# The last projection of a decode kernel in two half rows: two column groups, two PSUM banks, two copies, one store

## The chip, the cores and the metric

The kernel runs on one core of one Trainium2 chip. The metric is device time in microseconds for one launch; the median of several runs is compared. Beside the runs there is one profiled execution, from which all durations of single instructions come.

## What is computed

One decode step of a single token with 512 features. The token is normalised, goes through sliding-window attention over the last 4096 cached positions (32 query heads, 8 key and value heads of 128) and through a gated feed-forward part of 1792 hidden features, and everything is added up:

```
xn  = layernorm(x)                                   # 1 x 512
q   = xn @ wq                                        # 1 x 4096 = 32 heads of 128
o   = softmax(q k^T * 128**-0.5) v                   # last 4096 positions of the caches
A   = o @ wo                                         # 4096 x 512
r   = xn @ w_r                                       # one number
y   = (silu(xn @ w_gate) * (xn @ w_up)) @ w_down     # 512 x 1792, 512 x 1792, 1792 x 512
out = x + A + xn + y * sigmoid(r)                    # 1 x 512, bf16
```

With one token the choice among tokens in the reference always picks it, so the routed part is the plain sum above.

## The kernel before

All weights and the caches' window are read once from HBM, 30.67 MB, and the transfers are issued by SyncE (SP) in the order in which they are used: wq, keys, values, w_gate and w_up, wo, w_down. wo is read in four pieces of eight rows (of its 32) and w_down in five pieces of 4, 4, 3, 2 and 1 rows (of its 14); a row here is a block of 128 partitions by 512 columns, and row j multiplies column j of the transposed activation. Into the SBUF space of the keys go wo (`wo_sb`) and w_down (`wd_sb`), so their transfers are issued when the keys have been copied on.

The program is not scheduled by a planner: every engine has its own list of instructions in the order in which the Python code calls it, and the order between engines is kept by semaphores. `PE.mark(ins)` lets an instruction count up TensorE's semaphore and returns a token, and `DVE.need(token)` puts a wait for it into VectorE's list, ahead of everything that follows there. PE is TensorE, DVE is VectorE, ACT is ScalarE, POOL is GpSimd.

The stage that the change touches is the last one. All its matmuls have a stationary operand of a single column (one token), so each one yields a single row of output; to use more of the array, matmuls are placed with `tile_position` in one of four groups of 32 columns, where they write to PSUM partition 0, 32, 64 or 96. There are two patterns:

- `grouped` (L495): row j of a weight, all 512 columns, goes to column group j mod 4. Four rows of the weight run in four groups, and the sum over the groups is left for later. The target is `a_ps`, PSUM bank 5. The 32 rows of wo and the rows 0 to 7 of w_down are done like this.
- `by_columns` (L500): one row is cut into four pieces of 128 columns, and each piece goes to its own group, so nothing has to be added over the groups. The target is `g_ps`, 128 columns of PSUM bank 0. The rows 8 to 13 of w_down are done like this.

In between, at L517, DVE adds `rf` (which holds x + xn in partition 0 and zero elsewhere) to `a_ps` and leaves `part` in SBUF, fp32. PE then multiplies `part` by `sel4`, a column which has a one at partitions 0, 32, 64 and 96, through `by_columns` too: that adds the four groups up and brings them into `g_ps`. It stands in PE's list after the third piece of w_down (k == 2). Both banks are set to zero with a zero matmul ahead of the stage (L488, L489), and `fill` (L155) issues matmuls of zeros which only keep PE busy.

At the end DVE copies `g_ps`, 128 partitions by 128 columns, to `res` as bf16 (L527), and SP stores the four rows at partitions 0, 32, 64 and 96 as the 512 outputs (L529; the helper that issues all transfers is at L159). POOL waits for that store.

Of the kernel before, what the change touches and what calls it, by code (L numbers as in the profile page):

```python
# [38 lines left out]
def kernel(  # L39
# [15 lines left out]
    P = 128  # L55
    D = A_x.shape[2]
# [9 lines left out]
    FB = F // P  # L66
# [18 lines left out]
    kT = sb("kT", [P, 4, 1024], BF16)  # L85
# [8 lines left out]
    hTr = sb("hTr", [P, FB, 32], BF16)  # L94
# [5 lines left out]
    zst = sb("zst", [P, P], BF16)  # L100
    zmov = sb("zmov", [P, 512], BF16)
# [5 lines left out]
    sel4 = sb("sel4", [P, 1], F32)  # L107
# [13 lines left out]
    oT2 = sb("oT2", [P, RJ], BF16)  # L121
# [7 lines left out]
    ps = nc.alloc_psum_tensor("ps", [P, 8, 512], F32)  # L129
# [4 lines left out]
    pT_ps = ps[:, 0:2, :].bitcast(BF16)  # L134
    pv_ps = ps[:, 2, :]
    a_ps = ps[:, 5, :]
    g_ps = ps[:, 0, 0:P]
    rf = kT[:, 0, :].bitcast(F32)
    part = kT[:, 1, :].bitcast(F32)
    res = kT[:, 2, 0:P]  # L140

    wq_flat = wq_sb[:].rearrange("p a b -> p (a b)")
    wgu = wq_flat[:, 0:2 * KT * F]
# [1 line left out]
    wd_sb = k_flat[:, 0:FB * D]  # L145
    wo_sb = k_flat[:, FB * D:(FB + RJ) * D]

    S = lambda n: nc.alloc_semaphore(n)
    PE, ACT, DVE, POOL, SP = (Eng(nc, nc.tensor, "pe"), Eng(nc, nc.scalar, "act"), Eng(nc, nc.vector, "dve"),
                              Eng(nc, nc.gpsimd, "pool"), Eng(nc, nc.sync, "sp"))  # L150
    te, ac, ve, gp, sy = nc.tensor, nc.scalar, nc.vector, nc.gpsimd, nc.sync

    def fill(n):
        for _ in range(2 * n):
            te.matmul(ps[:, 7, :], lhsT=zst[:], rhs=zmov[:], start=True, stop=True)  # L155

    def dma(eng, name, out_, in_):
        s = S("d_" + name)
        eng.dma_start(out=out_, in_=in_).then_inc(s, 16)  # L159
        return (s, 16)  # L160
# [36 lines left out]
    a = DVE.mark(ve.bn_stats(out=stats[:], in_=xrow[:]))  # L197
# [6 lines left out]
    a = DVE.mark(ve.reciprocal(out=sml[:, 1:2], in_=sml[:, 0:1]))  # L204
# [5 lines left out]
    for kt in range(KT):  # L210
        ins = te.matmul(ps[:, 6, 256 + kt:257 + kt], lhsT=xn_row[:].rearrange("a (p k) -> a k p", k=KT)[:, kt, :],  # L211
                        rhs=ident_bf[0:1, 0:1], start=True, stop=True)
# [5 lines left out]
    with nc.allow_low_precision(reason="0/1 values are exact in bf16"):  # L218
# [4 lines left out]
                                     in_=ident_bf[:].rearrange("p (q h) -> p h q", h=2)))  # L223
# [23 lines left out]
    for kh in range(2):  # L247
# [4 lines left out]
        for hf in range(2):  # L252
            for kt in range(kh * KH, (kh + 1) * KH):
                for c in range(4):
                    ins = te.matmul(ps[32 * c:32 * c + 1, hf, :], lhsT=xnT[:, kt:kt + 1],  # L255
                                    rhs=wq_sb[:, kt, (4 * hf + c) * 512:(4 * hf + c + 1) * 512],
                                    start=(kt == 0), stop=(kt == KT - 1), tile_position=(0, 32 * c))
# [4 lines left out]
    for hf in range(2):  # L262
# [3 lines left out]
        for hl in range(4):  # L266
            ins = te.transpose(qT_ps[:, hl, :], q4[:, hf, hl * DH:(hl + 1) * DH], ident_bf[:])  # L267
# [76 lines left out]
    with te.Fori(1, 9) as i:  # L344
# [14 lines left out]
    wd_chunks = [(0, 4), (4, 8), (8, 11), (11, 13), (13, 14)]  # L359
    t_wd = [dma(sy, f"wd{k}", wd_sb[:, j0 * D:j1 * D], wd_v[:, j0 * D:j1 * D]) for k, (j0, j1) in enumerate(wd_chunks)]  # L360
# [4 lines left out]
    a = POOL.mark(gp.memset(rf, 0.0))  # L365
# [8 lines left out]
    a = DVE.mark(ve.reduce_max(out=gm[:], in_=ps[0:2, 6, 0:P].rearrange("a (q c) -> a c q", q=8), axis=AX.X))  # L374
# [6 lines left out]
                              start=True, stop=True))  # L381
# [6 lines left out]
    for h in range(2):  # L388
        PE.need(t_p[h])
        for k in range(8):  # L390
            ins = te.transpose(tp[:, h, k * P:(k + 1) * P], p_sb[:, h, k * P:(k + 1) * P], ident_bf[:])
# [39 lines left out]
    with te.Fori(1, 9) as i:  # L431
# [4 lines left out]
        for tl in range(4):  # L436
            ins = te.matmul(pv_ps[32 * tl:32 * tl + 32, :], lhsT=pTcur[:, tl].rearrange("p q e r -> p (q e r)"),  # L437
                            rhs=vin[:, 0].rearrange("p (q t) d -> p t q d", t=4)[:, tl],
                            start=True, stop=False, tile_position=(0, 32 * tl))
        ins.then_inc(pe_pva, 1)  # L440
        te.wait_ge(s_vb, i)
        for tl in range(4):
            ins = te.matmul(pv_ps[32 * tl:32 * tl + 32, :], lhsT=pTcur[:, 4 + tl].rearrange("p q e r -> p (q e r)"),  # L443
                            rhs=vin[:, 1].rearrange("p (q t) d -> p t q d", t=4)[:, tl],
                            start=False, stop=True, tile_position=(0, 32 * tl))
        ins.then_inc(pe_pv, 1)
        collect(psf[:, bass.ds(4 * 512 + g * 8, 8)]).then_inc(pe_col, 1)
        for _ in range(W3):
# [9 lines left out]
    a = DVE.mark(ve.reduce_sum(out=oT_f[:].rearrange("p (g j) -> p g j", g=HP),  # L458
                               in_=ps[:, 4, 8:72].rearrange("p (g u j) -> p g j u", g=HP, u=2), axis=AX.X))
# [7 lines left out]
    for m in range(2):  # L467
        PE.need(t_g if m == 0 else t_u)
        for kt in range(KT):
            for c in range(4):  # L470
                ins = te.matmul(ps[32 * c:32 * c + 1, 2 + m, 0:FC], lhsT=xnT[:, kt:kt + 1],
                                rhs=wgu[:, m * KT * F + kt * F + c * FC:m * KT * F + kt * F + (c + 1) * FC],
                                start=(kt == 0), stop=(kt == KT - 1), tile_position=(0, 32 * c))
# [6 lines left out]
    a = ACT.mark(ac.activation(out=gth4[:], in_=ps[:, 2, 0:FC], func=ACTF.Tanh, scale=0.5))  # L480
# [5 lines left out]
    DVE.need(t_h)  # L486
    t_hT = DVE.mark(ve.transpose(out=hTr[:].rearrange("p b i -> p (b i)"), in_=h4[:].rearrange("p b i -> p (b i)")))
    te.matmul(a_ps, lhsT=zst[:], rhs=zmov[:], start=True, stop=False, skip_group_check=True)  # L488
    te.matmul(g_ps, lhsT=zst[:], rhs=zmov[:, 0:P], start=True, stop=False, skip_group_check=True)  # L489
    fill(F4)  # L490
    PE.need(t_oT2)

    def grouped(j, lhsT, w):
        c = j % 4
        return te.matmul(a_ps[32 * c:32 * c + 1, :], lhsT=lhsT, rhs=w[:, j * D:(j + 1) * D], start=False, stop=False,  # L495
                         tile_position=(0, 32 * c), skip_group_check=True)

    def by_columns(lhsT, row, stop=False):
        for c in range(4):
            ins = te.matmul(g_ps[32 * c:32 * c + 1, :], lhsT=lhsT, rhs=row[:, c * P:(c + 1) * P], start=False, stop=stop,  # L500
                            tile_position=(0, 32 * c), skip_group_check=True)
        return ins

    for k, (j0, j1) in enumerate(wo_chunks):
        PE.need(t_wo[k])
        for j in range(j0, j1):
            grouped(j, oT2[:, j:j + 1], wo_sb)
        if k in (1, 2):
            fill(1)
    PE.need(t_hT)  # L510
    for k, (j0, j1) in enumerate(wd_chunks[:2]):
        PE.need(t_wd[k])
        for j in range(j0, j1):
            ins = grouped(j, hTr[:, j, 0:1], wd_sb)
    t_g4 = PE.mark(ins)
    DVE.need(t_g4, t_rf)
    t_part = DVE.mark(ve.tensor_tensor(out=part, in0=a_ps, in1=rf, op=ALU.add))  # L517
    for k, (j0, j1) in list(enumerate(wd_chunks))[2:]:
        PE.need(t_wd[k])
        for j in range(j0, j1):  # L520
            ins = by_columns(hTr[:, j, 0:1], wd_sb[:, j * D:(j + 1) * D], stop=(j == FB - 1))
        if k == 2:
            PE.need(t_part, t_sel4)
            by_columns(sel4[:], part)
    t_a = PE.mark(ins)
    DVE.need(t_a)
    t_res = DVE.mark(ve.tensor_copy(out=res, in_=g_ps))  # L527
    SP.need(t_res)
    t_out = dma(sy, "out", out.rearrange("a b (c d) -> (a b c) d", c=4), res[0:97:32, :])  # L529
    POOL.need(t_out)  # L530


# [28 lines left out]
```

## Time and profile before

| | |
|---|---|
| median of 7 runs | 82.12 us (81.96 to 82.23) |
| profiled execution | 81.92 us |
| its span, first to last instruction | 80.1 us |
| PE busy, matmul | 56.3 us (70% of the span) |
| DVE busy | 44.0 us (55%) |
| ACT busy | 30.1 us (38%) |
| POOL busy | 10.2 us (13%) |
| read from HBM | 30.67 MB, 383 GB/s over the span |
| mean granted clock of PE | 0.947 |

The span leaves out what lies before the first and after the last instruction: 81.92 less 80.1, or 1.8 us, belong to the execution but not to the span. The profiled execution is one of many and lies 0.2 us below the median. Busy shares are means over stages that have different limits, so they don't say what ends the kernel; that is read from the chain of waits. In the rows of a profile `128*1` after a matmul is the stationary operand, 128 rows by one column, then come output and input with partitions x elements and type, and `xN` is the number of instructions. `PEld` is the load of a stationary operand. `[0.59 <-DMA ...]` is idle time before the row and what ended it. `SPq` is the issue of a transfer, not the transfer.

### The profile page before, as it was taken

How to read it: one execution, taken by the hardware profiler on the slowest of the kernel's cores; microseconds unless marked ns; L12 is line 12 of the kernel's file. 1: busy time of each engine (PE TensorE's matmuls, PEld its weight loads, DVE VectorE, ACT ScalarE, POOL GpSimd, SP SyncE). 2: the span in 40 equal slices, each digit the busy share in tenths (PEclk: the TensorE clock that was granted, in tenths of full speed). 3: DMA queues.
4: the chain of work that ended last, by engine and by line, in shares of the span. 5: the costliest groups of instructions: out<-in, count | busy, mean ns of one | idle time of the engine just before them, and what ended most of it. 6: DMA issues, size and time to landing. Idle time of an engine off the chain costs nothing.

```text
span 80.1 us, 1607 instructions
## 1 busy us (share of the span) xinstructions
PE 56.3 (70%) x633; PEld 29.2 (36%) x633; DVE 44.0 (55%) x96; ACT 30.1 (38%) x40; POOL 10.2 (13%) x22
## 2 busy tenths in 40 slices
PE   0010973849999997997996786778887799537540
PEld 0010401236875865865864224222222353101120
DVE  3778100166538869668783662988989249200310
ACT  1941000502379789689568025222243320000000
POOL 5930000000102202202206900000000000000000
PEclk9999999999999999999999999999999999985555
DMA  0999998999999999999999999999999999999400
GB/s 1 319 434 417 401 474 368 442 433 466 425 401 474 425 409 409 466 417 409 458 413 417 401 483 401 403 439 444 429 401 424 409 429 421 409 405 398 158 1 1
DMA packets 3183, 30.72 MB, mean 383 GB/s; under 512 B 362, under 2 KB 492, under 8 KB 1004
## 3 DMA queue, kind: packets, MB, share of 16 engines
q1 hardware_dynamic: 3176, 30.67, 91.5%
q8 instruction: 2, 0.03, 0.2%
q14 instruction: 1, 0.01, 0.0%
q10 hardware_dynamic: 4, 0.00, 0.0%
HBM read 30.67 MB, written 0.00 MB: 383 GB/s over the span
## 4 chain that ended last, share of the span: by engine, by line
DMA 49%; PE 22%; SPq 17%; ACT 4%; DVE 3%; issue 2%
DMA k_sb<-in_B_w_down_dram 34%; SPq L159 17%; DMA wq_sb<-in_A_wq_dram 15%; PE ps L327 13%; ACT kT L302 4%; PE ps L336 4%; PE ps L255 2%; PE ps L500 2%; DVE kin L294 2%; PE ps L267 1%; DVE kT L299 1%; DVE qpad L272 1%; DVE kT L527 0%; SPq L556 0%; SPq L74 0%
## 5 line engine op out<-in xcount | busy, mean ns | idle before, releaser
L302 ACT COPY kT<-ps 128x1024 bf16<-128x1024 bf16 x19 | 18.6, 1015 | 9.6 <-PE ps L327 9.5
L327 PE MATMUL ps<-perm_bf,kin 128*128 128x128 bf16 x256 | 19.4, 237 | 1.2 <-DVE kin L294 0.9
L327 PEld LDWEIGHTS ps<-perm_bf,kin 128*128 128x128 bf16 x256 | 16.5, 107 | 5.7 <-issue 4.4
L294 DVE COPY kin<-k_sb 128x2048 bf16<-128x2048 bf16 x16 | 10.9, 686 | 3.3 <-PE ps L327 3.3
L299 DVE COPY kT<-ps 128x1024 bf16<-128x1024 bf16 x13 | 9.0, 691 | 3.9 <-PE ps L327 3.4
L422 ACT CAST pvS<-ps 128x512 bf16<-128x512 f32 x8 | 4.7, 585 | 10.0 <-PE ps L428 10.0
L336 PE MATMUL ps<-kT,qAB 128*32 128x512 bf16 x68 | 7.2, 415 | 1.6 <-ACT kT L302 1.5
L287 POOL COPY qAB<-qpad 128x64 bf16<-128x64 bf16 x8 | 3.5, 443 | 34.0 <-PE ps L336 34.0
L402 DVE COPY vin<-v_sb 128x2048 bf16<-128x2048 bf16 x8 | 5.5, 684 | 1.1 <-PE ps L437 1.0
L408 DVE COPY vin<-v_sb 128x2048 bf16<-128x2048 bf16 x8 | 5.5, 682 | 0.0
L437 PE MATMUL ps<-vin,pTcur 128*32 128x512 bf16 x32 | 3.2, 386 | 2.6 <-ACT pvS L422 2.2
L255 PE MATMUL ps<-wq_sb,xnT 128*1 128x512 bf16 x32 | 3.8, 620 | 1.7 <-DMA wq_sb<-in_A_wq_dram 1.7
L449 PE MATMUL ps<-zmov,zst 128*128 128x512 bf16 x16 | 4.7, 377 | 0.0
L272 DVE COPY qpad<-ps 128x16 bf16<-128x16 bf16 x4 | 0.5, 169 | 7.5 <-PE ps L267 7.5
L155 PE MATMUL ps<-zmov,zst 128*128 128x512 bf16 x16 | 4.5, 383 | 0.0
L517 DVE TENSOR_TENSOR kT<-ps,kT 128x512 f32<-128x512 f32 x1 | 0.7, 692 | 6.8 <-PE ps L495 6.8
L495 PE MATMUL ps<-k_sb,oT 128*1 128x512 bf16 x32 | 2.7, 436 | 2.2 <-DMA k_sb<-in_A_wo_dram 2.2
L261 ACT CAST q<-ps 128x512 bf16<-128x512 f32 x2 | 1.2, 585 | 6.7 <-PE ps L255 6.7
L211 PE MATMUL ps<-ident_bf,xn_row 1*128 1x1 bf16 x4 | 0.3, 166 | 4.8 <-POOL qAB L188 4.8
L443 PE MATMUL ps<-vin,pTcur 128*32 128x512 bf16 x32 | 3.2, 387 | 0.3 <-DVE vin L408 0.2
L336 PEld LDWEIGHTS ps<-kT,qAB 128*32 128x32 bf16 x68 | 1.9, 94 | 3.8 <-issue 1.5
L437 PEld LDWEIGHTS ps<-vin,pTcur 128*32 128x32 bf16 x32 | 1.1, 93 | 6.0 <-DVE vin L402 5.5
(97 smaller groups left out, 52.0 us busy)
## 6 DMA issues: line engine op xcount, KB each, us to landing
v_sb<-in_A_v_cache_dram SPq DMA_DIRECT2D x4, 2048.0 KB, 39.8
k_sb<-in_A_k_cache_dram SPq DMA_DIRECT2D x3, 2048.0 KB, 24.2
wq_sb<-in_A_wq_dram SPq DMA_DIRECT2D x2, 2048.0 KB, 9.7
k_sb<-in_A_wo_dram SPq DMA_DIRECT2D x4, 1024.0 KB, 32.6
k_sb<-in_A_k_cache_dram SPq DMA_DIRECT2D x2, 1024.0 KB, 14.8
wq_sb<-in_B_w_gate_dram SPq DMA_DIRECT2D x1, 1792.0 KB, 42.7
wq_sb<-in_B_w_up_dram SPq DMA_DIRECT2D x1, 1792.0 KB, 46.6
k_sb<-in_B_w_down_dram SPq DMA_DIRECT2D x2, 512.0 KB, 33.5
```

The lines of the kernel that those rows point to most:

```text
L155: te.matmul(ps[:, 7, :], lhsT=zst[:], rhs=zmov[:], start=True, stop=True)
L159: eng.dma_start(out=out_, in_=in_).then_inc(s, 16)
L255: ins = te.matmul(ps[32 * c:32 * c + 1, hf, :], lhsT=xnT[:, kt:kt + 1], rhs=wq_sb[:, kt, (4 * hf + c) * 512:(4 * hf + c + 1) * 512], start ...
L294: ve.tensor_copy(out=kin[:, 2 * h:2 * h + 2, :], in_=k_sb[:, g, 2 * h:2 * h + 2, :]).then_inc(s_c[h], 1)
L299: ve.tensor_copy(out=kT[:, b, :], in_=tp[:, b, :]).then_inc(s_ev[b], 1)
L302: ac.copy(out=kT[:, b, :], in_=tp[:, b, :]).then_inc(s_ev[b], 1)
L327: ins = te.transpose(tp[:, b, k * P:(k + 1) * P], kin[:, b, k * P:(k + 1) * P], perm_bf[:])
L336: ins = te.matmul(sc[32 * cq:32 * cq + 32, e, :], lhsT=qAB[:, e, :], rhs=kT[:, b, :].rearrange("d (k h q) -> d h k q", h=2, q=PH)[:, e], s ...
L402: ve.tensor_copy(out=vin[:, 0].rearrange("p (q k) d -> p q (k d)", q=4), in_=v_in[:, :, 0:4 * DH]).then_inc(s_va, 1)
L408: ve.tensor_copy(out=vin[:, 1].rearrange("p (q k) d -> p q (k d)", q=4), in_=v_in[:, :, 4 * DH:]).then_inc(s_vb, 1)
L422: ac.copy(out=pvS[:].rearrange("p t d -> p (t d)"), in_=pv_ps).then_inc(s_pvs, 1)
L449: te.matmul(ps[:, 7, :], lhsT=zst[:], rhs=zmov[:], start=True, stop=True)
```

## The change

The whole of w_down now goes through one pattern, `by_halves`: a row is cut into two halves of 256 columns, and half c goes to column group c (PSUM partition 32c) in a PSUM bank of its own (bank c). `grouped` is left with the rows of wo. The addition at L517 comes right after these, and the matmuls of `part` with `sel4` come after the first piece of w_down (k == 0) instead of the third. Two zero matmuls of 256 columns set up the two banks. At the end DVE copies half 0 and ACT half 1, both to partition 0 of `res`, and SP stores 512 values from that partition in one piece. Transfers into the core, their order and all that comes before this stage stay as they are.

```
--- before.py
+++ after.py
@@ -134,10 +134,11 @@
     pT_ps = ps[:, 0:2, :].bitcast(BF16)
     pv_ps = ps[:, 2, :]
     a_ps = ps[:, 5, :]
-    g_ps = ps[:, 0, 0:P]
+    HD = D // 2
+    g_ps = [ps[32 * c:32 * c + 1, c, 0:HD] for c in range(2)]
     rf = kT[:, 0, :].bitcast(F32)
     part = kT[:, 1, :].bitcast(F32)
-    res = kT[:, 2, 0:P]
+    res = kT[0:1, 2, 0:D]
 
     wq_flat = wq_sb[:].rearrange("p a b -> p (a b)")
     wgu = wq_flat[:, 0:2 * KT * F]
@@ -486,7 +487,8 @@
     DVE.need(t_h)
     t_hT = DVE.mark(ve.transpose(out=hTr[:].rearrange("p b i -> p (b i)"), in_=h4[:].rearrange("p b i -> p (b i)")))
     te.matmul(a_ps, lhsT=zst[:], rhs=zmov[:], start=True, stop=False, skip_group_check=True)
-    te.matmul(g_ps, lhsT=zst[:], rhs=zmov[:, 0:P], start=True, stop=False, skip_group_check=True)
+    for c in range(2):
+        te.matmul(ps[:, c, 0:HD], lhsT=zst[:], rhs=zmov[:, 0:HD], start=True, stop=False, skip_group_check=True)
     fill(F4)
     PE.need(t_oT2)
 
@@ -495,38 +497,36 @@
         return te.matmul(a_ps[32 * c:32 * c + 1, :], lhsT=lhsT, rhs=w[:, j * D:(j + 1) * D], start=False, stop=False,
                          tile_position=(0, 32 * c), skip_group_check=True)
 
-    def by_columns(lhsT, row, stop=False):
-        for c in range(4):
-            ins = te.matmul(g_ps[32 * c:32 * c + 1, :], lhsT=lhsT, rhs=row[:, c * P:(c + 1) * P], start=False, stop=stop,
+    def by_halves(lhsT, row, stop=False):
+        for c in range(2):
+            ins = te.matmul(g_ps[c], lhsT=lhsT, rhs=row[:, c * HD:(c + 1) * HD], start=False, stop=stop,
                             tile_position=(0, 32 * c), skip_group_check=True)
         return ins
 
     for k, (j0, j1) in enumerate(wo_chunks):
         PE.need(t_wo[k])
         for j in range(j0, j1):
-            grouped(j, oT2[:, j:j + 1], wo_sb)
+            ins = grouped(j, oT2[:, j:j + 1], wo_sb)
         if k in (1, 2):
             fill(1)
-    PE.need(t_hT)
-    for k, (j0, j1) in enumerate(wd_chunks[:2]):
-        PE.need(t_wd[k])
-        for j in range(j0, j1):
-            ins = grouped(j, hTr[:, j, 0:1], wd_sb)
     t_g4 = PE.mark(ins)
     DVE.need(t_g4, t_rf)
     t_part = DVE.mark(ve.tensor_tensor(out=part, in0=a_ps, in1=rf, op=ALU.add))
-    for k, (j0, j1) in list(enumerate(wd_chunks))[2:]:
+    PE.need(t_hT)
+    for k, (j0, j1) in enumerate(wd_chunks):
         PE.need(t_wd[k])
         for j in range(j0, j1):
-            ins = by_columns(hTr[:, j, 0:1], wd_sb[:, j * D:(j + 1) * D], stop=(j == FB - 1))
-        if k == 2:
+            ins = by_halves(hTr[:, j, 0:1], wd_sb[:, j * D:(j + 1) * D], stop=(j == FB - 1))
+        if k == 0:
             PE.need(t_part, t_sel4)
-            by_columns(sel4[:], part)
+            by_halves(sel4[:], part)
     t_a = PE.mark(ins)
     DVE.need(t_a)
-    t_res = DVE.mark(ve.tensor_copy(out=res, in_=g_ps))
-    SP.need(t_res)
-    t_out = dma(sy, "out", out.rearrange("a b (c d) -> (a b c) d", c=4), res[0:97:32, :])
+    ACT.need(t_a)
+    t_r0 = DVE.mark(ve.tensor_copy(out=res[:, 0:HD], in_=g_ps[0]))
+    t_r1 = ACT.mark(ac.copy(out=res[:, HD:], in_=g_ps[1]))
+    SP.need(t_r0, t_r1)
+    t_out = dma(sy, "out", out.rearrange("a b d -> (a b) d"), res)
     POOL.need(t_out)
```

## The prediction

> **What bounds the kernel now.** I read the chain of waits first, then the DMA issues, then the last microseconds of the timeline, and last the table of engine time by stretch for the granted clock. The chain:
>
> ```profile
> DMA 49%; PE 22%; SPq 17%; ACT 4%; DVE 3%; issue 2%
> 48.41 27.27 DMA k_sb<-in_B_w_down_dram
> 75.72 1.39 PE ps L500 x26
> 77.14 0.29 DVE kT L527
> ```
>
> The reader is to see that the end hangs on the arrival of w_down, and that after it come only 1.39 us of TensorE (PE), one copy and the store. The change touches nothing ahead of 66 us that could move a transfer, so all is decided between the arrivals and the end. The issues of the last three pieces of w_down, with size and time to landing (the last row shows when the last was issued):
>
> ```profile
> k_sb<-in_B_w_down_dram SPq DMA_DIRECT2D x1, 384.0 KB, 27.3
> k_sb<-in_B_w_down_dram SPq DMA_DIRECT2D x1, 256.0 KB, 23.6
> k_sb<-in_B_w_down_dram SPq DMA_DIRECT2D x1, 128.0 KB, 20.1
> 56.52 3.26 SPq L159 DMA_DIRECT2D k_sb<-in_B_w_down_dram  x1
> ```
>
> Issue plus landing gives the arrivals: piece 4 at 56.52 + 20.1 = 76.62; piece 3 (issued 52.76) at 76.36; piece 2 (48.41) at 75.71; in the same way piece 1 (44.12 + 30.6) at 74.72 and piece 0 (37.06 + 36.4) at 73.46. What the engines do then:
>
> ```profile
> 74.78 0.59 PE L495 MATMUL ps<-k_sb,hTr 128*1 128x512 bf16 x4 [0.59 <-DMA k_sb<-in_B_w_down_dram]
> 75.42 0.69 DVE L517 TENSOR_TENSOR kT<-ps,kT 128x512 f32<-128x512 f32 x1 [6.79 <-PE ps L495]
> 75.72 0.49 PE L500 MATMUL ps<-k_sb,hTr 128*1 128x128 bf16 x12 [0.35 <-DMA k_sb<-in_B_w_down_dram]
> 76.17 0.61 PE L500 MATMUL ps<-kT,sel 128*1 128x128 f32 x8
> 76.55 0.55 PE L500 MATMUL ps<-k_sb,hTr 128*1 128x128 bf16 x12
> 77.14 0.29 DVE L527 CAST kT<-ps 128x128 bf16<-128x128 f32 x1 [1.02 <-PE ps L500]
> 77.46 0.66 SPq L159 DMA_DIRECT2D out_dram<-kT  x1
> ```
>
> The last twelve matmuls are rows 11, 12 and 13 of w_down, four each, so a row takes 0.11 us and row 13 starts at 76.55 + 2 x 0.11 = 76.77, only 0.15 after its data landed. PE keeps up with the transfers with little to spare. The stretches show at which clock:
>
> ```profile
> core 0: us, PE busy (x) PEld busy (x) DVE busy (x) ACT busy (x) POOL busy (x), PEclk, DMA share, GB/s
> 71.00:72.00 1.00, 0.00 (x0) 0.00 (x0) 0.00 (x0) 0.00 (x0) 0.00 (x0) 0.86 1.02 406
> 76.00:77.00 1.00, 1.00 (x28) 0.47 (x20) 0.12 (x1) 0.00 (x0) 0.00 (x0) 0.50 0.01 4
> ```
>
> PE idles from 70.85 to 72.20; the clock falls to 0.50 in that gap (0.86 over the stretch puts it near 71.7 to 71.9) and stays there. The tail is run at half clock.
>
> **What the Trainium skill says.** "TensorE: Matmul & The Clock Gate", Part 1, has the clock binary, 1.2 or 2.4 GHz, decided over a free-running window of about 3.4 us; the trace agrees in the two values 1.00 and 0.50. Its section "Back-to-back issue gap" gives N / 1.2 ns when cold: 107 ns for 128 columns, against the 0.11 us per row here. "DMA: Bandwidth & Descriptors", Specifications, says that transfers under 512 B are read-modify-write; the trace shows the store's 8 packets, all under 512 B, but not that step. "PSUM — Partial Sum Buffer", Specifications, lets VectorE and ScalarE read PSUM in parallel if the banks differ, as the two halves' banks do; the trace has no such pair to show it.
>
> **The change, part by part.**
>
> *Matmuls of a row.* Before, L500 spreads 512 columns over four column groups, 128 each, at once: 0.11 us per row. After, two groups take 256 each, so a row takes 256 / 128 x 0.107 = 0.213 us at half clock, and two groups stand idle. Rows 0 to 7 also change form: L495 ran four rows side by side at 512 columns (0.427 for four, 0.107 a row). All 14 rows thus cost double, 14 x 0.213 = 2.99 us.
>
> *The addition of the partial sums.* The DVE step at L517 no longer waits for pieces 0 and 1 but only for wo, whose last matmuls run from 72.20 to 73.22. It takes 0.69, so it is done near 74.0. Nothing is queued behind it on DVE but the final copy. The fp32 matmuls with sel4 follow piece 0. Before they ran from 76.17 to the next start at 76.55, 0.38 for 128 columns; at 256 columns 0.76, or by the cold rate for two half-rate passes 0.85. I take 0.76. What was saved is a detour on PE at 76.2 which delayed row 13 by at most the 0.15 above.
>
> *PE's queue, laid end to end at half clock.* Piece 0 starts as now at 73.59: four rows, 0.85, to 74.44. part is ready at 74.0, so no wait: sel4 to 75.20. Piece 1 (here since 74.72) 0.85 to 76.05. Piece 2 (since 75.71) 0.64 to 76.69. Piece 3 (since 76.36) 0.43 to 77.12. Row 13 (since 76.62) starts at 77.12 instead of 76.77: PE no longer waits for DMA at all but for itself. A matmul of 128 columns lasts 0.304 (mean at L500), one of 512 0.586 (mean of the hTr rows at L495), so one of 256 about 0.304 + 0.282 / 3 = 0.40. The end moves from 77.10 to 77.12 + 0.40 + 0.01 = 77.53: **+0.43 us**. Bounds: +0.52 with the dearer sel4, and -0.05 if PE were warm throughout (row 13 at 76.7 and a shorter matmul).
>
> *The zeroing at L489.* Two matmuls of 256 columns instead of one of 128 at full clock, some 0.16 us more at 66.2. Costed at nothing: between the matmuls of wo's second and third pieces PE idles over 0.8 us for DMA (68.82 to 69.71). Without that cover it would be 0.16.
>
> *The copy.* Before, one DVE copy of 128 columns, 0.290. A copy of 32 columns (L478, also out of PSUM, also a cast) took 0.191, so 1.03 ns a column; 256 columns cost 0.290 + 128 x 1.03 = 0.42. ScalarE does 512 columns in 0.585 (L422); from 1.015 for 1024 a column is worth 0.84 ns, so its half takes 0.585 - 0.215 = 0.37, and DVE is the later: **+0.13**. Fewer partitions save nothing, since the time goes with columns. SP now waits for both; behind that wait is only the store, and POOL waits for the store alone. Bounds: +0.08 (both at the ScalarE price) to +0.20 (the second semaphore or ScalarE's start is late).
>
> *The store.* Before: four rows of 256 B from four partitions, issue 0.66 at 77.46, its packets from 78.70, that is 1.24 after issue. After: one row of 1 KB from one partition. Nearest is the load of x, one row of 1 KB: issued at 0.91 in 0.50, packet near 1.79, 0.88 after issue. If the store became like that, it would save 0.36; if the cost is the store's own, nothing; one engine moving 1 KB instead of four moving 256 B could cost 0.1. I take **-0.20**, with -0.36 and +0.10 as ends.
>
> Sum: 0.43 + 0.13 - 0.20 = **+0.36 us**. The profiled execution took 81.92 (span 80.1 and 1.82 around it), 0.20 below the median 82.12, so it would become 82.28, and the median 82.12 + 0.36 = **82.48**.
>
> **The rivals.**
>
> *PE is not the bound, because the clock is up for part of the tail.* The window is free-running, so its edge can fall elsewhere in other executions: the drop could come as late as about 74.6, one window after the earliest edge that could still find PE idle enough. Then piece 0 and sel4 run warm (done near 74.37 instead of 75.20) and only from piece 1 on is PE cold: 74.76 to 75.61, piece 2 from its arrival to 76.39, piece 3 to 76.82, row 13 from there: end near 77.23, +0.13. The dense queue could also win the clock back after a full busy window, near 77 and too late. Against it: this execution fell at 71.8, and any edge before 73.6 gives the whole +0.43. Time: 82.12 + 0.13 + 0.13 - 0.20 = 82.18, no change.
>
> *The store is worth more than all the rest costs (faster).* If a write under 512 B really reads first, one row of 1 KB drops that read. The price by the nearest row is x's, from packet (1.79) to its first use on DVE (2.27), 0.48; with the 0.36 at issue 0.84 is saved: 0.56 - 0.84 = -0.28, 81.84. It decides from a saving of 0.72. For it: 1.35 us lie between the store's packets and the end of the span, more than an ordinary read takes. Against: no row shows a store of 512 B or more, and a write's acknowledgment may fill that time alone.
>
> *The change does nothing, as the transfers hide it.* They hide work before 76.62; the sum above finds 3.75 us of PE between 73.59 and 77.3, so they can't.
>
> **How the numbers follow.** PE-bound as worked out: 0.64, with 82.30 to 82.80 as its own range. Clock up for part: 0.18. Store decisive: 0.18. A measurement of this kernel can tell about 0.2%, 0.16 us, from no change: faster ends at 81.96, slower begins at 82.28. The second rival gives faster in most of its chance (0.17), the first is split (0.15 within, the rest slower), some of the PE-bound case with the full saving at the store stays within. So faster 0.17, same 0.18, slower 0.65. The range: 81.90 leaves out most of the faster case, 82.85 leaves out a sum of all upper ends.
>
> **What would show it.** Right: L500's bf16 rows 0.213 apart with no DMA wait ahead of pieces 2 to 4, at PEclk 0.50; the sel4 group 0.76 before the next start; row 13 starting 0.4 or more after its landing; the DVE copy at 0.42 and ScalarE's at 0.37; the store's issue well under 0.66. Wrong: PE waiting for DMA at piece 4, rows 0.11 apart, or over 0.7 us won between the store's issue and the end.

## The result, and the profile after

The changed kernel takes 81.64 us (median, 81.26 to 82.25) against 82.05 us before: ratio 0.9956, 95% interval 0.9945 to 0.9966, or 0.41 us less. The forecast was 82.48, slower. A later repeat gave 81.77 against 82.06, ratio 0.9966 (0.9950 to 0.9982), or 0.28 less.

The profiled execution took 81.68 (span 79.9). Its chain of waits, shares and then the last pieces (start us, length, what):

```profile
DMA 60%; PE 21%; ACT 7%; DVE 4%; SPq 2%; issue 2%
35.63 36.57 DMA k_sb<-in_A_wo_dram
72.90 0.70 DVE kT L514
73.63 3.65 PE ps L502 x32
77.30 0.41 DVE kT L526
```

From 73.63 on it is PE alone, 3.65 us, as the forecast laid it out. The step ahead of it is not to be taken as shown: the chain puts PE's start at 73.63 down to the addition at L514, and so leads back to wo, but in the program the rows of w_down's first piece don't wait for the addition, only the sel4 matmuls after them do. That piece landed at 73.49 by the trace's record, just ahead, and in a run below the same rows start at 73.64 while the addition ends at 74.04. So w_down's first piece starts the stage, and PE sets its end. The timeline (start us, length, instruction, idle time before it and what ended it):

```profile
73.63 1.02 PE L502 MATMUL ps<-k_sb,hTr 128*1 128x256 bf16 x8 [0.78 <-DVE kT L514]
74.43 1.06 PE L502 MATMUL ps<-kT,sel 128*1 128x256 f32 x4
75.29 1.97 PE L502 MATMUL ps<-k_sb,hTr 128*1 128x256 bf16 x20
77.30 0.36 ACT L527 CAST kT<-ps 1x256 bf16<-1x256 f32 x1 [12.36 <-PE ps L502]
77.30 0.41 DVE L526 CAST kT<-ps 1x256 bf16<-1x256 f32 x1 [3.71 <-PE ps L502]
77.75 0.32 SPq L160 DMA_DIRECT2D out_dram<-kT  x1
```

And the issue of the last piece of w_down on SP's queue, with the row of the table of transfers that gives its time to landing:

```profile
56.56 3.26 SPq L160 DMA_DIRECT2D k_sb<-in_B_w_down_dram  x1
k_sb<-in_B_w_down_dram SPq DMA_DIRECT2D x1, 128.0 KB, 20.3
```

Four things are to be seen. The sel4 group holds PE from 74.43 to 75.29, 0.86 us. The ten rows after it start without any wait for DMA. The copies take 0.41 and 0.36, as forecast. The store's issue takes 0.32 instead of 0.66.

Two differences below are so small that the rounding of the views to 0.1 us (time to landing, span) matters, so they are taken from the times that the traces themselves hold. Piece 4 landed at 76.82 here, 0.17 later than in the execution of before (76.65). PE ended 0.44 after that landing in both, where the forecast had it later by 0.43 than before. From the end of the DVE copy to the end of the span it is 2.18 us, and was 2.71: 0.53 saved at the store. The clock in two short stretches of the same execution:

```profile
core 0: us, PE busy (x) PEld busy (x) DVE busy (x) ACT busy (x) POOL busy (x), PEclk, DMA share, GB/s
73.30:73.35 0.05, 0.00 (x0) 0.00 (x0) 0.05 (x1) 0.00 (x0) 0.00 (x0) 0.73 1.15 451
...
76.70:76.75 0.05, 0.05 (x4) 0.00 (x0) 0.00 (x0) 0.00 (x0) 0.00 (x0) 0.64 0.00 0
```

The clock fell in a gap of PE (0.73 in the stretch shown, 1.00 ahead of it and 0.50 after it), later than in the execution of before, and came back at 76.74, 3.4 us later. The Trainium skill names a free-running window of about 3.4 us ("TensorE: Matmul & The Clock Gate", Part 1); the two edges agree with it. Row 13 ran at full clock, and started 0.16 after its landing, where the forecast named 0.4 or more as a sign of being right.

### The profile page after: what moved, and what is told of

It is laid out like the page before. It is cut to its first block, busy times and chain, and to the rows that moved or that the text cites. A ratio compares the mean times of both kernels' runs of the same rounds, so it can differ in the third digit from the quotient of the medians.

```text
span 79.9 us, 1595 instructions
## 1 busy us (share of the span) xinstructions
PE 55.8 (70%) x626; PEld 29.6 (37%) x626; DVE 44.2 (55%) x96; ACT 30.3 (38%) x41; POOL 10.1 (13%) x22
## 4 chain that ended last, share of the span: by engine, by line
DMA 60%; PE 21%; ACT 7%; DVE 4%; SPq 2%; issue 2%
DMA k_sb<-in_A_wo_dram 46%; DMA wq_sb<-in_A_wq_dram 15%; PE ps L328 10%; ACT kT L303 6%; PE ps L502 5%; PE ps L337 3%; SPq L160 2%; DVE kin L295 2%; PE ps L268 1%; DVE kT L514 1%; DVE kT L300 1%; PE ps L256 1%; PE ps L497 1%; ACT q L262 1%; DVE qpad L273 1%
## 5 line engine op out<-in xcount | busy, mean ns | idle before, releaser
L256 PE MATMUL ps<-wq_sb,xnT 128*1 128x512 bf16 x32 | 2.9, 499 | 1.5 <-DMA wq_sb<-in_A_wq_dram 1.5
L514 DVE TENSOR_TENSOR kT<-ps,kT 128x512 f32<-128x512 f32 x1 | 0.7, 692 | 5.2 <-PE ps L497 5.2
L502 PE MATMUL ps<-k_sb,hTr 128*1 128x256 bf16 x28 | 3.0, 381 | 0.8 <-DVE kT L514 0.8
```

What stands on the lines that cost most here:

```text
L502: ins = te.matmul(g_ps[c], lhsT=lhsT, rhs=row[:, c * HD:(c + 1) * HD], start=False, stop=stop, tile_position=(0, 32 * c), skip_group_check ...
```

## The experiments

The kernel before ran beside each group of experiments. Its medians were 82.07 beside the store alone, two rows, four pieces and the clock held up; 82.13 beside sixteen pieces, the clock let down, the zero matmuls in the kernel before and the order alone; 82.06 beside the two repeats, both copies on DVE and the two stores. Ratios are to the kernel before of the same group, and totals of different groups are compared by them.

**The store alone.** Only the store of the kernel before is changed:

```
+ row0 = kT[0:1, 2, 0:D]
- out.rearrange("a b (c d) -> (a b c) d", c=4), res[0:97:32, :]
+ out.rearrange("a b d -> (a b) d"), row0
```

> The kernel before with nothing changed but the store: one row of 512 values from partition 0 instead of four rows of 128 values from four partitions (three quarters of the stored values are therefore not the result). Theory 1 (the store is worth most of the change: in the two profiles 2.67 us from the end of the DVE copy to the end of the span became 2.19): faster by 0.4 to 0.5 us, about 81.6, issue of the store 0.32 us instead of 0.66. Theory 2 (the store's form is worth the 0.20 us of the prediction and the rest of the gain came from PE): faster by about 0.2 us. Theory 3 (the gain is all at PE, where the addition no longer stands between the rows): no change.

Measured: 81.46, ratio 0.9930 (0.9908 to 0.9953), 0.57 us less, with 0.39 to 0.75 as interval. The store's row on SP's queue:

```profile
77.52 0.32 SPq L160 DMA_DIRECT2D out_dram<-kT  x1
```

The packets follow 0.75 us after the issue began (78.27) instead of 1.25, and from the packets to the end of the span it is 1.4 us as before (78.27 to 79.7, 78.71 to 80.1). The saving lies between the start of the issue and the packets, not in the write: 0.34 of it in the issue itself, the other 0.17 between the end of the issue and the packets (78.11 to 78.71 before, 77.84 to 78.27 here). From the end of the copy to the end of the span it is 2.18 us, as in the changed kernel. Theory 1 holds, theories 2 and 3 fall: the store alone is worth at least about the whole gain of the change.

**Two rows of 512 B.** The changed kernel, with the halves on partitions 0 and 32:

```
- res = kT[0:1, 2, 0:D]
+ res = kT[:, 2, 0:HD]
- out=res[:, 0:HD], in_=g_ps[0]
+ out=res[0:1, :], in_=g_ps[0]
- out=res[:, HD:], in_=g_ps[1]
+ out=res[32:33, :], in_=g_ps[1]
- out.rearrange("a b d -> (a b) d"), res
+ out.rearrange("a b (c d) -> (a b c) d", c=2), res[0:33:32, :]
```

> The changed kernel, but the two copies write to partitions 0 and 32, and the store takes two rows of 512 B. Theory 1a (the price goes with the size of a piece, under 512 B or not): as the changed kernel, 81.6, since 512 B is enough. Theory 1b (the price goes with the number of rows and engines): in between, 81.75 to 81.9, issue near 0.45 us. If the store is worth nothing: no difference from the changed kernel, issue unchanged.

Measured: 82.21, ratio 1.0021 (1.0005 to 1.0037), issue 0.64:

```profile
77.81 0.64 SPq L160 DMA_DIRECT2D out_dram<-kT  x1
```

Theories 1a and 1b both fail: two rows are about as dear as four, and 512 B doesn't help. From the end of the copies to the end of the span it is 2.67, with the four rows of before 2.71.

**Four and sixteen pieces from one partition.** The result lies on partition 0 with gaps, and the store takes it in pieces of 256 B or of 64 B:

```
+ res = kT[0:1, 2, :].rearrange("a (c d) -> a c d", c=4)[:, :, 0:P]       # or c=16, 0:32
+ out.rearrange("a b (c d) -> (a b) c d", c=4), res                       # or c=16
```

> The changed kernel, but the result lies on partition 0 in four pieces with gaps, and is stored as four pieces of 256 B from that one partition. Theory 1a (size of a piece) and theory 1b (number of pieces): slower than the changed kernel by the whole 0.48 us, about 82.1, with 8 packets and an issue near 0.66 us. Theory 1c (the number of partitions that the store reads): as the changed kernel, 81.6.

> The changed kernel with its result on partition 0 in sixteen pieces of 32 values with gaps, stored as sixteen pieces of 64 B. If the issue is dear for any count of rows over one: 0.64 to 0.76 us or more of issue, about 82.2. If it is dear only for counts between one and sixteen (the transfers of 128 rows took 0.33): issue 0.33, about 81.65. If it goes with the number of rows: over 1 us of issue, 82.5 or more.

Measured: 82.18, ratio 1.0025 (1.0008 to 1.0042), issue 0.76, for four pieces; 82.34, ratio 1.0039 (1.0022 to 1.0056), issue 0.61, for sixteen. The number of partitions is not the cause, and neither is the number of pieces beyond one. On SP's queue:

```profile
77.40 0.76 SPq L160 DMA_DIRECT2D out_dram<-kT  x1
```

This is the issue of four pieces, and the next one that of sixteen:

```profile
77.68 0.61 SPq L160 DMA_DIRECT2D out_dram<-kT  x1
```

One row costs 0.32 to issue, 2 to 16 short ones 0.61 to 0.76. From the end of the copies to the end of the span, which leaves out all that PE does, it is 2.82 for four pieces and 2.84 for sixteen, against 2.18 for one row.

**A load of four rows, and the store of four rows twice.** Two kernels, run once each, ask what the dear issue belongs to:

```
+ SP.need(t_part)                                             # in the changed kernel
+ dma(sy, "x4", kin[0:97:32, 3, 0:P], A_x.rearrange("a b (c d) -> (a b c) d", c=4))
+ SP.need(t_oT2)                                              # in the kernel before
+ dma(sy, "o4", out.rearrange("a b (c d) -> (a b c) d", c=4), kin[0:97:32, 3, 0:P])
```

> The changed kernel with one more transfer on SP's queue after the addition: a load of x as four rows of 256 B, which nothing uses. If the dear issue belongs to stores: this load's issue takes about 0.33 us. If it belongs to several short rows in either direction: 0.6 us or more. The final store of one row stays at 0.32.

> The kernel before with one more store of four rows of 256 B, issued by SP once the activations for wo are ready, with contents that the final store overwrites; the final store waits for it. If the dear issue is a first use: the second store's issue takes about 0.33 us. If not: 0.66 again. The total may be longer, since the extra store queues behind the loads.

Measured: 81.42 and 82.16 in one run each, beside 81.89 for the kernel before; single runs say little of the total, so only the issues are read. The load's issue on SP's queue:

```profile
73.60 0.64 SPq L160 DMA_DIRECT2D kin<-in_A_x_dram  x1
```

And both stores of the other kernel:

```profile
65.44 0.66 SPq L159 DMA_DIRECT2D out_dram<-kin  x1
77.64 0.56 SPq L159 DMA_DIRECT2D out_dram<-kT  x1
```

A load of four short rows is as dear as a store, so the direction is not the cause. In the other kernel the first store costs 0.66 and the second still 0.56, so a first use is at most a small part. Still open is what the sequencer does in that time, and why a load of 128 rows of 8 KB (wo, 0.33 for the first piece) is as cheap as one row; no run here tells whether it is the count or the length of the rows.

**The clock held up.** The changed kernel with more zero matmuls in PE's waits for wo:

```
- if k in (1, 2):
-     fill(1)
+ fill((0, 2, 3, 1)[k])
```

> The changed kernel with zero matmuls put into PE's waits for wo, 4, 6 and 2 of them after the second, third and fourth piece instead of 2, 2 and none, so that the clock is held up in the tail. Theory C (with the clock at half speed the changed kernel is bound by PE, and executions where the clock falls late or comes back early are not): faster than the changed kernel by 0.1 to 0.2 us in the median, near 81.5, the runs above 81.9 gone, PE waiting for DMA ahead of the last rows, rows 0.107 apart. Rival (PE is hidden behind the transfers either way): the same 81.64 and the same spread.

> The changed kernel itself, for comparison on the same chip: 81.64, from 81.3 to 82.2.

> The changed kernel with the clock held up once more beside the changed kernel on the same chip. Theory C: 0.1 to 0.2 us faster in the median than the changed kernel, and a spread under 0.4 us where that has 0.8 or more. Rival: no difference.

Measured: 81.56 (81.42 to 81.61), ratio 0.9935 (0.9918 to 0.9952), and in the repeat 81.54 (81.41 to 81.65), 0.9932 (0.9913 to 0.9952), beside the changed kernel itself with 81.77 (81.36 to 82.37). Theory C holds: the median is lower by 0.2 in the same group, and all twelve runs of the two lie within 0.24, where the 22 of the changed kernel spread over 1.0. By its median this is the quickest kernel of the study that computes the whole result. Its timeline in the repeat, whose trace has the clock up until 78.14:

```profile
74.08 0.60 PE L502 MATMUL ps<-kT,sel 128*1 128x256 f32 x4
...
75.87 0.49 PE L502 MATMUL ps<-k_sb,hTr 128*1 128x256 bf16 x6 [0.44 <-DMA k_sb<-in_B_w_down_dram]
...
76.53 0.59 PE L502 MATMUL ps<-k_sb,hTr 128*1 128x256 bf16 x6 [0.17 <-DMA k_sb<-in_B_w_down_dram]
76.85 0.08 PEld L502 LDWEIGHTS ps<-k_sb,hTr 128*1 128x1 bf16 x2 [0.23 <-DMA k_sb<-in_B_w_down_dram]
```

PE waits for DMA again, down to the single row of piece 4.

**The clock let down.** The changed kernel without the zero matmuls between wo's pieces:

```
- if k in (1, 2):
-     fill(1)
```

> The changed kernel without the zero matmuls between the pieces of wo, so that the clock falls earlier, and a busy stretch long enough to win it back before the last row becomes unlikely. Theory C (the prediction's +0.43 us at PE is right where the whole tail is at half clock): 81.9 to 82.1, 0.3 to 0.5 slower than the changed kernel, rows 0.213 apart to the end. Rival (PE hidden either way): 81.64.

Measured: 81.89 (81.35 to 82.27), ratio 0.9968 (0.9950 to 0.9986). The expected 0.3 to 0.5 is not shown by the median: it lies 0.25 above the 81.64 of the changed kernel, but that was another group, and by the ratio it can't be told from the changed kernel's repeat (0.9966). The executions are mixed: 10 of 22 took 82.0 or more, against 4 of 26 and 6 of 22 for the changed kernel. The profiled one is of the kind that the forecast described, at half clock to the end:

```profile
73.35 0.69 DVE L512 TENSOR_TENSOR kT<-ps,kT 128x512 f32<-128x512 f32 x1 [4.66 <-PE ps L497]
73.64 1.02 PE L502 MATMUL ps<-k_sb,hTr 128*1 128x256 bf16 x8 [0.35 <-DMA k_sb<-in_B_w_down_dram]
74.45 1.06 PE L502 MATMUL ps<-kT,sel 128*1 128x256 f32 x4
75.30 2.35 PE L502 MATMUL ps<-k_sb,hTr 128*1 128x256 bf16 x20
77.68 0.36 ACT L525 CAST kT<-ps 1x256 bf16<-1x256 f32 x1 [11.74 <-PE ps L502]
```

The ten rows after sel4 take 2.35 to their end instead of 1.97. By the trace's times PE ends 0.93 after piece 4's landing, where before it was 0.44. So the loss at PE is 0.49, near the upper bound of 0.52 that the forecast gave with the dearer sel4.

Profiles put side by side show how often the clock does this: six of the other runs here have the same matmuls, zero matmuls included, as the changed kernel and differ only at the copies, the store or an extra load. The granted clock in 40 slices of the span, in tenths of full speed (9 stands for 90% or more), for the changed kernel, the sixteen pieces, the load of four rows, and last the run of this section:

```profile
PEclk9999999855599999999999999999999999998579
PEclk9999999999999999999999999999999999995696
PEclk9999999755599999999999999999999999999999
PEclk9999999999999999999999999999999999985555
```

In the seven profiles with the changed kernel's matmuls the clock fell during the stage in four (at 73.32 in the changed kernel, 73.33 in its repeat, 73.95 with two rows, 72.32 with sixteen pieces), and was back 3.41 us later each time. PE then ended 0.44, 0.53, 0.57 and 0.32 after piece 4's landing. In the other three (four pieces, load of four rows, both copies on DVE) it stayed up until PE was done, which was 0.32 after the landing each time. None was at half clock to the end. Here, with a fall at 71.72, the stage was.

**The same zero matmuls in the kernel before.**

> The kernel before with the same zero matmuls in PE's waits as in the run of the changed kernel with the clock held up. Theory C (PE matters only in the changed kernel, whose rows cost double): no more than 0.1 us faster than before, 82.0, because before row 13 starts 0.15 us after its landing at half clock already. Rival (the clock itself is worth as much in either kernel): faster by 0.2 to 0.4 us.

Its edit is the one above, `fill((0, 2, 3, 1)[k])`, in the kernel before. Measured: 81.92, ratio 0.9977 (0.9968 to 0.9987), 0.19 less, with 0.11 to 0.26 as interval. Theory C's limit of 0.1 fails, and the rival's 0.2 lies within the interval: the clock is worth about as much in either kernel. In its profile PE ends 0.32 after piece 4's landing, 0.13 less than before, which lies within the interval too. With the clock held up in both kernels, what is left of the change is, by the ratios, 0.34 and 0.37 us; the store less the dearer copy gives 0.53 - 0.12 = 0.41.

**The order alone.** The changed kernel's order with all rows through four groups, and the copy and the store of before:

```
- for k, (j0, j1) in enumerate(wd_chunks[:2]): ... grouped(j, hTr[:, j, 0:1], wd_sb)
- for k, (j0, j1) in list(enumerate(wd_chunks))[2:]:
+ for k, (j0, j1) in enumerate(wd_chunks):                    # by_columns for all rows
- if k == 2:
+ if k == 0:                                                  # sel4 after piece 0
```

> The order of the changed kernel (addition after wo, sel4 after piece 0) with all 14 rows through four column groups of 128, and the copy and the store of the kernel before. It gives what the order alone is worth. Prediction's step (the addition between the rows delayed row 13 by at most 0.15 us): 0 to 0.1 us faster than before, 81.95 to 82.05. Rival (the order is where the gain lies): 81.7 or less.

Measured: 81.97, ratio 0.9986 (0.9978 to 0.9994), 0.11 less, with 0.05 to 0.18 as interval. PE waits for DMA ahead of the last row. From its timeline:

```profile
76.53 0.61 PE L500 MATMUL ps<-k_sb,hTr 128*1 128x128 bf16 x12 [0.16 <-DMA k_sb<-in_B_w_down_dram]
76.86 0.09 PEld L500 LDWEIGHTS ps<-k_sb,hTr 128*1 128x1 bf16 x4 [0.23 <-DMA k_sb<-in_B_w_down_dram]
```

The granted clock was 0.50 in the last three of its page's forty slices, and still PE was in time, done 0.32 after the landing: in this order rows over four groups are hidden at half clock, while rows over two, at half clock to the end, were not (0.93).

**The copies, and the store from two queues.** DVE copies both halves in the first; in the second, with the clock held up, SP stores the half that DVE copied and ScalarE the half that it copied itself:

```
+ t_r1 = DVE.mark(ve.tensor_copy(out=res[:, HD:], in_=g_ps[1]))       # instead of ac.copy
+ t_o0 = dma(sy, "out0", row[:, 0:HD], res[:, 0:HD])                  # second kernel
+ t_o1 = dma(ac, "out1", row[:, HD:], res[:, HD:])
```

> The changed kernel with both halves copied by DVE, one after the other. If the copies lie on the path with nothing beside them: slower than the changed kernel by a second copy, 0.35 to 0.41 us, about 82.0. If ScalarE's start or the second semaphore is the dearer part of the changed kernel: less than 0.3 slower.

> The changed kernel with the clock held up, and the store cut into two single rows of 512 B, one issued by SP after DVE's copy, one by ScalarE after its own. If an issue is cheap whenever it is a single row: both at 0.2 to 0.5 us, total 81.5 to 81.6, at most 0.05 better, since the store then waits for one copy instead of two. If two stores at once disturb each other or ScalarE's queue is slow at its first store: 81.7 to 82.0.

Measured: 82.15, ratio 1.0011 (0.9995 to 1.0028), 0.38 above the changed kernel in the same group; and 81.57, 0.9936 (0.9918 to 0.9955), the same as with one store. The copies lie on the path in full, and ScalarE's half saves a whole second copy. Two single rows are both cheap to issue (0.23 on ScalarE's queue, 0.32 on SP's), and nothing is won.

## Why the prediction was wrong, point by point

The forecast was +0.36 us and the measure -0.41, 0.77 apart. Two terms of the sum make this up: PE's queue and the store.

*What bounds the kernel* was right: all was decided after 73.5 us, and PE took over from DMA where the clock was down.

*PE's queue* is the step that failed. The +0.43 was worked out for a tail at half clock to the end, that case was given a chance of 0.64, and the ground was that any fall of the clock before 73.6 gives the whole of it, since the clock would be back "near 77 and too late". In the profiled execution the clock fell at 73.32, was back at 76.74, before rows 11 to 13, and PE's end moved by -0.01 against piece 4's landing. Some of that is luck, since piece 4 came late there; in the repeat, with the same fall and return, it moved by +0.08. Falls from 72.32 to 73.95 gave from -0.13 to +0.13, and only the one at 71.72 gave +0.49. For the case that it was meant for, the sum was right in form and nearly in size (sel4 was taken at 0.76 and took 0.86); the case turned out rare, not likely.

*The store* is the term that was mis-sized: 0.20 was taken, and the traces have 0.53. The run of the store alone gives 0.57 with an interval that holds it. The nearest row, x's load, pointed to 0.36, and I halved that on the ground that it could be the store's own cost. Even the full 0.36 was too little.

With these two put right the sum is -0.01 + 0.12 - 0.53 = -0.42 by the two profiles. The rival in which the store decides ended on the right side, but by luck: it kept the +0.43 at PE, needed more than 0.72 saved at the store to decide, and built that on a read ahead of a short write. The Trainium skill states such a read for under 512 B ("DMA: Bandwidth & Descriptors", Specifications); here rows of 512 B cost about as much as rows of 256 B, and the time from packets to the end was 1.39 us against 1.42. Nearly all of the saving is ahead of the packets.

The runs fit two cases. With the store put right, they come out at 82.05 + 0.49 + 0.12 - 0.53 = 82.13 for half clock to the end and, with PE in time, at 82.05 - 0.12 + 0.12 - 0.53 = 81.52 (the first 0.12 is what the order saves at PE by the profile of the order alone, 0.44 less 0.32). The second is what the runs with the clock held up show (81.56 and 81.54), and the median lies between them. Of the 28 executions of the changed kernel for which a mean clock is listed, four took 82.02 or more, and their mean clock was 0.946 to 0.953; the profile at half clock to the end in the run with the clock let down has 0.947. That those four were such executions is likely, not shown: the mean also falls by a dip earlier in the kernel, as the changed kernel's own profile has (slices 9 to 11 of its clock above), and executions with a mean of 0.935 and 0.936 took only 81.68 to 81.77.

*The order* was costed as at most 0.15 of delay to row 13 and put at nothing in the sum of the likeliest case, where PE is late anyway. With PE in time it is worth 0.11.

*The copy* was right: 0.42 and 0.37 predicted, 0.413 and 0.363 measured. *The zeroing* at L491 was put at nothing, and nothing speaks against it: the gap ahead of wo's last piece still ends on DMA (1.34 us). No run isolates it.

## What to carry to other kernels

Price the last store by what lies ahead of its packets: count the rows of its access pattern, and ask what it takes to bring the result into a single row before anything else in the tail is trimmed. A matmul stage whose rows use half the column groups cost double here, and whether that showed depended on when the clock fell; a few zero matmuls in the waits ahead of the stage were worth 0.2 us in either kernel, and in the changed one they took away the long executions. When the state of a resource at a fixed point decides the sign, one profiled execution gives one draw of it, not its distribution; a few more profiles of the same instructions would have given the share that the forecast had to guess.

## What the runs showed of the hardware that was not expected

- Issuing one row took 0.29 to 0.32 us on SP's queue, 2, 4 and 16 short rows 0.56 to 0.76, in loads and stores alike, whatever the row's size (64 to 512 B) and whether they came from one partition or several; the packets of a store moved about 0.75 us after the issue of one row began and about 1.2 us or more after that of several. On ScalarE's queue single rows took 0.23 (half of the result) and 0.50 (x, the first transfer there), so the price of one row is not the same on every queue.
- In the four profiles where the clock fell during the stage with the changed kernel's matmuls, it was back 3.41 us later.
- An fp32 matmul of a single stationary column over two groups took 0.86 us for two pieces of 256 columns at half clock, 0.38 for four pieces of 128 over four groups before: more than double for the doubled columns. A bf16 row of two pieces of 256 took 0.213, so fp32 took four times that.
